# Opening loads and TensorE order of a fused attention and gated-FFN kernel: another load order, and a planner that prefers the tile shape that is on

## The chip, the cores and the metric

The kernel runs on one core of a Trainium2 chip. The metric is the device time of one execution in microseconds (us); lower is better. Before the change the median of three runs is 578.52 us (577.92 to 578.53). The five engines of the core are written as in the profile: PE (TensorE; PEld are its weight loads), DVE (VectorE), ACT (ScalarE), POOL (GpSimd) and SP (SyncE, which here only issues DMAs).

## The reference

All inputs are bfloat16; S = 2048 tokens, D = 576, 32 heads of 18, a window of 256 tokens, F = 4608.

```python
def _A_ref(x, wqkv, wo):                       # sliding-window attention
    qkv = (x @ wqkv).reshape(B, S, 3, H, Dh)   # ... to q, k, v by head
    scores = einsum("bhqd,bhkd->bhqk", q, k) * (Dh ** -0.5)
    mask = (idx[:, None] - idx[None, :] >= 0) & (idx[:, None] - idx[None, :] < W)
    p = softmax(where(mask, scores, -1e9))
    return einsum("bhqk,bhkd->bhqd", p, v) ... @ wo
def _B_ref(x, w_gate, w_up, w_down):           # gated FFN
    return (sigmoid(x @ w_gate) * (x @ w_up)) @ w_down

xn = layernorm(x)
return x + _A_ref(xn, wqkv, wo) * silu(_B_ref(xn, w_gate, w_up, w_down))
```

## The kernel before

The tokens are done in four chunks of 512 (`NCH`, `CH`), each of four tiles of 128 (`QPC`). The 576 features are split into nine blocks of 64 (`NC`), and most matmuls contract over 64 rows: two of them, one on the upper and one on the lower half of the array, run side by side. So PE works in four tile shapes, which the code calls modes: `full` (128 rows: the down projection F2, the transposes of the opening, the dummy matmuls), `r64` (64 rows: QKV projections, the output projection `wo`, gate and up matmuls F1), `r32` (32 rows: attention scores) and `c32` (32 columns: probabilities times V).

For a chunk the work is, by name: layer norm of four tiles (`bn1`, `bn2`, `ag`, `ve`, `rstd`, `apply`, `wrap`; lines 388 to 405, mostly DVE); the transposed normalised tile into `xn`, in chunk 0 by PE transposes `tr` (L424) and ACT copies `xe`, in later chunks by DMA transposes `xt`; twelve projections (`qk:c:i:0` is q of tile i, `qk:c:i:1` is k, `v:n` is v; L446, 18 matmuls each); for q and k an evacuation into a ring of three buffers `pk`, from which a DMA transpose `qkt` (L201) makes `qkp`; attention by eight groups of four heads (`sc` scores, L536; `pv`, L615); F1 for 36 tiles of 128 hidden features in weight groups of three (`fa:c:t`, `fb0`, `fb1`; L723, 18 matmuls per tile; the weights of group g are `w:c:g`, four DMAs); the output projection (`wo:c:0`, `wo:c:0s`, `wo:c:1`, `wo:c:1s`; L680); F2 for four token tiles in nine steps each (`f2:tile:step`; L791, in the last tile L821); and the final combination (`fth` on ACT, L852; `fq1`, `fq2`, `fq3` on DVE, L854 to L858), after which `out` is stored. `wo:c:0s` may start only when the results of `wo:c:0` have arrived (a fence), and `wo:c:1s` after `wo:c:1`. `fq2` of tile i needs `se` (L695), the ACT evacuation of its `wo`. Projection q of tile 3 (`qk:0:3:0`) writes a `pk` buffer that the transpose `qkt` of q of tile 2 must have read; `fa:0:3` is the first user of weight group 1.

Nothing of the order is written out by hand. `build` makes operations with dependencies, a priority, and a duration in ns that the author set by constants; `schedule` (L864) is a list planner: at each step it takes for every engine the operation with the least start time plus `prio * PRIO_NS`, and among the engines the earliest. The result is one fixed program per engine, and on the chip each engine runs its program strictly in that order, waiting on semaphores. So a changed constant moves no work by itself, but can give another order on every engine, SP included: SP issues all loads, stores and DMA transposes of the kernel, one after the other.

The constants that matter here: `MODE_NS` is added when PE goes to another mode (L957); `X_PRIO`, `QKV_LOAD` and `W0_PRIO` are the priorities of the opening loads (four tiles of x, twelve DMAs of `wqkv`, four of weight group 0); `W_FACTOR` scales the bytes that the planner counts for a `wqkv` load. `WARM` puts ten dummy matmuls (L327) at the start of PE's program, and `WARM_MORE` one more after the transposes of each of tiles 0 and 1. Loads of x for the final sum go into a ring of two buffers `xf` and wait for the store that empties the buffer; the planner adds `LATE_SLACK` (5000 ns) to their arrival.

Of the kernel before, what the change touches and what calls it, by code (L numbers as in the profile page):

```python
# [8 lines left out]
D = 576  # L9
# [3 lines left out]
P = 128  # L13
# [17 lines left out]
NC = D // 64  # L31
# [3 lines left out]
RW = 3  # L35
# [26 lines left out]
SEM_NS = 50.0  # L62
DMA_SLACK_NS = 600.0
PE_TAIL = 166.0
MODE_NS = 112.0
BEGIN_NS = 800.0
DMA_ISSUE_NS = 440.0
W_ISSUE_NS = 660.0
# [3 lines left out]
LN_STEP = 1  # L72
WARM = 10
X0_SLACK = 0.0
WARM_MORE = (1, 1)
X_PRIO = (-9, -9, -7, -5)
QKV_LOAD = (-8, -4, -6)
W0_PRIO = -3
WARM_NS = 427.0
W_FACTOR = 1.35  # L80
XT_BYTES = 1.6
DMA_LAT_NS = 1600.0
DMA_BYTES_PER_NS = 320.0
# [21 lines left out]

class Op:
    __slots__ = ("eng", "occ", "lat", "deps", "fn", "name", "prio", "start", "done", "tok",
                 "needs_tok", "nbytes", "idx", "slack", "succs", "cidx", "odeps", "alloc", "mode", "lane", "fence")

    def __init__(self, eng, occ, fn, name, deps, prio, nbytes=0, odeps=(), alloc=(), mode=None, lane=None):  # L110
        self.eng = eng
        self.occ = float(occ)
        self.lat = {"PE": PE_TAIL, "ACT": 110.0, "DVE": 85.0, "POOL": 50.0, "SP": 0.0}[eng]
        self.fn = fn
        self.name = name
        self.deps = []
        for d in deps:
            self.add_dep(d)
        self.prio = prio
        self.start = None  # L120
        self.done = None
        self.tok = None
        self.needs_tok = False
        self.nbytes = nbytes
        self.idx = -1
        self.succs = []
        self.odeps = [d for d in odeps if d is not None]
        self.alloc = list(alloc)
        self.mode = mode
        self.lane = lane  # L130
        self.fence = None

    def add_dep(self, d):
        if d is None:
# [27 lines left out]
class Builder:  # L162
# [156 lines left out]
        self.warm(WARM, "warm:0", [self.op_pre])  # L319
        self.op_pkz = op("ACT", 1300 + 1900, lambda e: e.memzero(self.pk[:, :, :, :]), "pkz", prio=0)  # L320

    def warm(self, n, name, deps, odeps=()):
        ps = Psum((3,))

        def f(e):
            for k in range(n):
                r = e.matmul(self.bank(ps), self.hT[:, 0, 0:P], self.hT[:, 0, :], start=True, stop=True)  # L327
            return r
        self.op_warm = self.pe(n * WARM_NS, f, name, deps=deps, prio=-9, psum=[ps], odeps=odeps)

    def load9(self, low, up, w_low, w_up, name, lane, deps, prio, factor=1.55):
        cols = w_low.shape[1]
# [39 lines left out]
    def build_ln(self, c):  # L372
        op = self.op
        pr = 0 if c == 0 else 2
        _, dxn = self.r_xn.take()
        self.op_xn = [[] for _ in range(QPC)]
        for i in range(QPC):
            st = c * QPC + i
            if c == 0:
                pr = LN_STEP * (i - QPC)  # L380
            ring, buf = (self.r_xf, self.xf) if c == 0 and i >= NXR else (self.r_xr, self.xr)
            sx, dx = ring.take()
            xs = buf[:, sx, :]
            o_x = self.dma(xs, self.x[st * P:(st + 1) * P, :], P * D * 2, f"x{st}",
                           ("x", i if c == 0 else sx), deps=dx + ([self.op_f1[(c - 1, 6 + 3 * i)]] if c > 0 else []),
                           prio=X_PRIO[i] if c == 0 else 4, slack=X0_SLACK if c == 0 else LATE_SLACK)
            sb_, db_ = self.r_bn.take()
            b1 = op("DVE", 360, lambda e, sb_=sb_, xs=xs: e.bn_stats(self.bnst[:, sb_, 0, :], xs[:, 0:288]),  # L388
                    f"bn1:{st}", deps=[o_x] + db_, prio=pr)
            b2 = op("DVE", 360, lambda e, sb_=sb_, xs=xs: e.bn_stats(self.bnst[:, sb_, 1, :], xs[:, 288:576]),  # L390
                    f"bn2:{st}", deps=[o_x] + db_, prio=pr)
            ag = op("DVE", 120, lambda e, st=st, sb_=sb_: e.bn_aggr(self.mv[:, st, :], self.bnst[:, sb_, :, :]),
                    f"ag:{st}", deps=[b1, b2], prio=pr)
            self.r_bn.release(sb_, ag)
            ve = op("DVE", 100, lambda e, st=st: e.tensor_scalar(self.veps[:, st, :], self.mv[:, st, 1:2], EPS,
                                                                None, ALU.add), f"ve:{st}", deps=[ag], prio=pr)
            rs = op("POOL", 560, lambda e, st=st: e.tensor_tensor(self.rstd[:, st, :], self.veps[:, st, :],  # L397
                                                                 self.neghalf[:, :], ALU.pow),
                    f"rstd:{st}", deps=[ve, self.op_negh], prio=0)
            sr, dr = self.r_xnr.take()  # L400
            ap = op("DVE", 350, lambda e, st=st, xs=xs, sr=sr: e.tensor_scalar(
                self.xnr[:, sr, 0:D], xs, self.mv[:, st, 0:1], self.rstd[:, st, :],
                ALU.subtract, ALU.mult), f"apply:{st}", deps=[rs, ag] + dr, prio=pr)
            ring.release(sx, ap)
            wr = op("DVE", 100, lambda e, sr=sr: e.tensor_copy(self.xnr[:, sr, D:DP], self.xnr[:, sr, 0:64]),
                    f"wrap:{st}", deps=[ap], prio=pr)
            tok = slice(i * P, (i + 1) * P)
            if c > 0:
                for k, (i0, i1, col) in enumerate(((0, NKT, 0), (NKT, NC, 64))):
                    o = self.dma(self.xn[:, i0:i1, tok], self.xnr[:, sr, col:col + (i1 - i0) * P],  # L410
                                 XT_BYTES * (i1 - i0) * P * P * 2, f"xt:{st}.{k}", ("xt", i, k), deps=[wr, ap] + dxn,
                                 prio=-2, issue=XT_ISSUE_NS, transpose=True)
                    self.r_xnr.release(sr, o)
                    self.op_xn[i].append(o)
                continue
            halves = [(0, NKT, 0), (NKT, NC, 64)]
            for i0, i1, col in halves:
                n = i1 - i0
                ps = Psum((4,), (5,), (6,), (7,), (0,), (1,), (2,), (3,))

                def f_tr(e, sr=sr, ps=ps, n=n, col=col):
                    b = ps.banks[0] * 1024
                    for k in range(n):
                        r = e.transpose(self.psb[:, b + k * P:b + (k + 1) * P],  # L424
                                        self.xnr[:, sr, col + k * P:col + (k + 1) * P], self.op_[:, NOT - 1, 0:P])
                    return r
                tr = self.pe(n * 58, f_tr, f"tr:{st}", deps=[wr, ap, self.op_ident] + dxn, prio=pr, psum=[ps])
                self.r_xnr.release(sr, tr)

                def f_xe(e, i=i, ps=ps, i0=i0, n=n):  # L430
                    b = ps.banks[0] * 1024
                    src = self.psb[:, b:b + n * P].rearrange("p (k c) -> p k c", k=n)
                    return e.activation(self.xn[:, i0:i0 + n, i * P:(i + 1) * P], src, ACTF.Copy)
                if i < len(WARM_MORE) and i1 == NC:
                    self.warm(WARM_MORE[i], f"warm:{i + 1}", [], [tr])
                self.op_xn[i].append(self.rd("ACT", act_ns(n * P), f_xe, f"xe:{st}", deps=[tr], prio=pr, psum=[ps]))
        self.all_xn = [o for l in self.op_xn for o in l]

# [76 lines left out]
    def build_attn(self, c, hg):  # L515
# [7 lines left out]
        masks = []  # L523
        for u, pieces in enumerate(units):
# [3 lines left out]
            ps = Psum((0, 1, 2, 3))  # L528
# [15 lines left out]
            pend = self.pending if u == PV_WITH else None  # L544
            if pend:
                self.pending = None
                o = self.pe(pend[1] + MODE_NS + nblk * P / 2.4 + 40, lambda e, a=pend[0], b=f_sc: (a(e), b(e))[1],
                            f"pvsc:{c}:{hg}:{u}", deps=pend[2] + deps, prio=0, psum=[pend[3], ps], mode=("c32", "r32"))
                pend[4](o)
            else:  # L550
                o = self.pe(nblk * P / 2.4 + 40, f_sc, f"sc:{c}:{hg}:{u}", deps=deps, prio=1, psum=[ps], mode="r32")
            self.op_sc[c][hg].append(o)
            exps = []
            for pr in range(2):
# [53 lines left out]
        def f_pv(e, ps=ps, where=where):  # L608
# [7 lines left out]
                                 self.expr[:, es, j, pos * P:(pos + n) * P], start=(m == 0), stop=(m == len(runs) - 1),  # L616
                                 tile_position=(0, 32 * j))
            return r
        self.pending = (f_pv, ncol / 2.4 + 40, masks + vdeps, ps, lambda o: self.after_pv(c, hg, ps, o, used))
        if hg == NHG - 1:  # L620
            o = self.pe(ncol / 2.4 + 40, f_pv, f"pv:{c}:{hg}", deps=masks + vdeps, prio=0, psum=[ps], mode="c32")
            self.pending[4](o)
            self.pending = None

# [75 lines left out]
    def build_ffn(self, c):  # L700
# [25 lines left out]
        for ft in range(NFT + 1):  # L726
            if ft < NFT:
                if ft % FG == 0:
                    fg = ft // FG
                    sw, dw = self.r_w.take()  # L730
                    slots.append(sw)
                    wp = (fg + 1 if fg else W0_PRIO) if c == 0 and fg < RW else -2
                    fc = slice(fg * FG * P, (fg + 1) * FG * P)
                    dmas.append(self.load9(self.wgs[0:64, sw, :, :], self.wgs[64:P, sw, :, :], self.wg[:, fc],
                                           self.wu[:, fc], f"w:{c}:{fg}", ("w", sw),
# [128 lines left out]
    def schedule(self):  # L864
# [14 lines left out]
        mode = "full"  # L879
# [31 lines left out]
        while n < total:  # L911
            best = None
            for e in ENGS:
                bo = None
                for o in enabled[e]:
                    st = max(free[e], ready[o.cidx])
                    pen = o.prio * PRIO_NS
                    if o.alloc:
                        if bo is not None and (st + pen, o.cidx) >= bo[0]:
                            continue  # L920
# [175 lines left out]
```

## Time and profile before

| what | before |
|---|---|
| median of three runs (lowest, highest) | 578.52 us (577.92, 578.53) |
| the profiled execution: its time, its span | 579.13 us, 577.1 us |
| PE busy | 568.1 us, 98% of the span |
| ACT, DVE, POOL busy | 303.3, 296.2, 24.4 us |
| F1 matmuls (L723) | 2592, 298.9 us busy |
| F2 matmuls (L791) | 1080, 135.8 us busy |
| projections (L446) | 864, 55.6 us busy |
| DMA traffic | 72.82 MB, mean 126 GB/s, 58.4% of 16 engines |

The span runs from the first to the last instruction of the profiled execution; the 2.0 us between it and that execution's time lie around it. The busy time of PE counts overlapping matmuls once, and the ends of matmuls are modelled, so a short wait or a change of tile shape does not show as idle time: start-to-start times have to be read instead. In the views below the columns are start, duration, engine, line, operation, destination and sources, count, and in brackets the idle time before it with what ended it.

### The profile page before, as it was taken

Reading aid. Unit: us, or ns where it says so; the run is one execution under the profiler, and the core shown is the slowest. Engines: PE = TensorE matmul, PEld = TensorE weight load, DVE = VectorE, ACT = ScalarE, POOL = GpSimd, SP = SyncE. Lnnn points to the kernel's source line nnn. Section 1 sums busy time; section 2 is a strip of 40 time slices with the busy share of each in tenths; the row PEclk is TensorE's granted clock in tenths of the full one; section 3 lists DMA queues with packets and bytes.
Section 4 is the critical chain, followed back from the end, with each engine's and each line's share of the span. In section 5 each row is a group of like instructions: output and inputs, shape, how many; then the busy total and the mean of one; then the engine's idle time right before and its main releaser. Section 6 shows DMA issues by size and latency. Waiting matters only on the chain.

```text
span 577.1 us, 14818 instructions
## 1 busy us (share of the span) xinstructions
PE 568.1 (98%) x6352; PEld 273.9 (47%) x6352; DVE 296.2 (51%) x589; ACT 303.3 (53%) x411; POOL 24.4 (4%) x51
## 2 busy tenths in 40 slices
PE   7999999999999999999999999999999999999996
PEld 4544334447544444455754444445564444444554
DVE  5237988403147887721225698761312677675012
ACT  5357887213168788530327878742133878882201
POOL 2001110000001010000000011000000000000000
PEclk9999999999999999999999999999999999999999
DMA  8999889634956664342693656544179356551010
GB/s 196 202 202 243 215 205 206 158 51 77 220 88 145 144 155 120 77 87 51 112 217 70 141 128 146 124 100 83 31 164 191 73 124 135 136 124 42 1 41 22
DMA packets 124861, 72.82 MB, mean 126 GB/s; under 512 B 53630, under 2 KB 124286, under 8 KB 124798
## 3 DMA queue, kind: packets, MB, share of 16 engines
q1 hardware_dynamic: 124798, 71.90, 58.4%
q8 instruction: 50, 0.82, 0.6%
q14 instruction: 13, 0.11, 0.1%
HBM read 55.22 MB, written 2.36 MB: 100 GB/s over the span
## 4 chain that ended last, share of the span: by engine, by line
PE 95%; DMA 2%; SPq 2%; DVE 1%; issue 0%; POOL 0%; ACT 0%
PE ps L723 50%; PE ps L791 23%; PE ps L446 8%; PE ps L536 5%; PE ps L615 4%; PE ps L680 3%; PE ps L821 2%; SPq L202 1%; DMA qkp<-pk 1%; DMA xf<-in_A_x_dram 1%; DVE pk L488 0%; SPq L201 0%; PE ps L424 0%; POOL rstd L397 0%; DVE bnst L388 0%
## 5 line engine op out<-in xcount | busy, mean ns | idle before, releaser
L723 PE MATMUL ps<-xn,wgs 64*128 64x512 bf16 x2592 | 298.9, 377 | 0.3 <-ACT pk L489 0.3
L558 ACT ACTIVATE expr<-ps 128x1024 bf16<-128x1024 f32 (+2 forms) x192 | 175.8, 968 | 39.9 <-PE ps L536 39.2
L723 PEld LDWEIGHTS ps<-xn,wgs 64*128 64x128 bf16 x2592 | 119.7, 94 | 150.1 <-issue 15.1
L791 PE MATMUL ps<-wd_sb,hT 128*128 128x512 bf16 (+1 forms) x1080 | 135.8, 287 | 0.0
L709 ACT ACTIVATE tring<-ps 128x512 bf16<-128x512 f32 x144 | 86.3, 599 | 68.5 <-PE ps L723 65.8
L713 DVE SCALAR_TENSOR_TENSOR hT<-tring,ps 128x512 bf16<-128x512 bf16 x144 | 97.2, 675 | 39.4 <-ACT tring L709 26.3
L592 DVE TENSOR_TENSOR expr<-expr,m 128x1024 bf16<-128x1024 bf16 (+1 forms) x152 | 82.4, 572 | 59.6 <-ACT expr L558 59.4
L791 PEld LDWEIGHTS ps<-wd_sb,hT 128*128 128x128 bf16 x1080 | 67.9, 98 | 66.6 <-issue 4.1
L854 DVE SCALAR_TENSOR_TENSOR thf<-thf,ps 128x576 bf16<-128x576 bf16 (+2 forms) x17 | 12.2, 719 | 97.6 <-ACT thf L852 97.6
L852 ACT ACTIVATE thf<-ps 128x576 bf16<-128x576 f32 (+2 forms) x17 | 10.6, 623 | 90.5 <-PE ps L791 82.9
L446 PE MATMUL ps<-wqkv_sb,xn 64*128 64x288 bf16 x864 | 55.6, 283 | 0.2 <-DMA qkp<-pk 0.2
L446 PEld LDWEIGHTS ps<-wqkv_sb,xn 64*128 64x128 bf16 x864 | 41.3, 94 | 13.6 <-issue 1.7
L536 PE MATMUL ps<-qkp 18*128 18x384 bf16 (+2 forms) x704 | 36.8, 276 | 0.0
L488 DVE CAST pk<-ps 128x576 bf16<-128x576 f32 x16 | 12.1, 755 | 39.9 <-PE ps L446 39.9
L630 DVE STREAM_TRANSPOSE tf<-ps 128x512 f32<-128x512 f32 x32 | 22.9, 716 | 13.5 <-PE ps L536 10.4
L536 PEld LDWEIGHTS ps<-qkp 18*128 18x128 bf16 x704 | 11.1, 92 | 34.6 <-issue 20.2
L489 ACT ACTIVATE pk<-ps 128x576 bf16<-128x576 f32 x16 | 10.4, 652 | 30.4 <-PE ps L446 30.4
L615 PE MATMUL ps<-expr,vau 128*32 128x256 bf16 (+2 forms) x704 | 25.6, 277 | 0.0
L597 POOL COPY qkp<-qkp 128x256 bf16<-128x256 bf16 x24 | 11.7, 489 | 308.2 <-PE ps L536 308.2
L644 DVE STREAM_TRANSPOSE op__63<-pk 128x512 bf16<-128x512 bf16 x32 | 22.7, 709 | 1.3 <-DVE pk L638 0.5
L695 ACT ACTIVATE sat<-ps 128x576 bf16<-128x576 f32 x16 | 9.2, 654 | 21.5 <-PE ps L680 21.5
L615 PEld LDWEIGHTS ps<-expr,vau 128*32 128x32 bf16 x704 | 13.1, 96 | 15.4 <-ACT tring L709 7.6
(39 smaller groups left out, 157.1 us busy)
## 6 DMA issues: line engine op xcount, KB each, us to landing
wgs<-in_B_w_gate_dram SPq DMA_DIRECT2D x48, 240.0 KB, 3.8
wgs<-in_B_w_up_dram SPq DMA_DIRECT2D x48, 240.0 KB, 4.7
wgs<-in_B_w_up_dram SPq DMA_DIRECT2D x48, 192.0 KB, 4.1
wgs<-in_B_w_gate_dram SPq DMA_DIRECT2D x48, 192.0 KB, 4.6
wd_sb<-in_B_w_down_dram SPq DMA_DIRECT2D x9, 576.0 KB, 5.0
xf<-in_A_x_dram SPq DMA_DIRECT2D x18, 144.0 KB, 2.3
out_dram<-xf SPq DMA_DIRECT2D x15, 144.0 KB, 2.0
xr<-in_A_x_dram SPq DMA_DIRECT2D x14, 144.0 KB, 4.4
```

Of the source, the lines that this page charges most:

```text
L446: r = e.matmul(self.bank(ps, HV, hf), self.xn[r0:r0 + 64, k, i * P:(i + 1) * P], self.wqkv_sb[r0:r0 + 64, j, k, :], start=(k == 0), stop=( ...
L536: r = e.matmul(self.ps[:, b:b + n * P], self.qkp[r0:r0 + DH, hg, k0:k0 + P], self.qkp[r0:r0 + DH, hg, q0 * P:(q0 + n) * P], start=True, st ...
L558: return e.activation(self.expr[:, es, 2 * pr:2 * pr + 2, 0:nblk * P], src, ACTF.Exp, scale=SM_SCALE)
L592: return e.tensor_tensor(ap, ap, m, ALU.mult)
L615: r = e.matmul(self.ps[32 * j:32 * j + 32, b + q0 * P:b + (q0 + n) * P], vf[:, v0:v0 + 32], self.expr[:, es, j, pos * P:(pos + n) * P], st ...
L630: t1 = self.rd("DVE", dve_ns(CH), lambda e, ps=ps: e.transpose(tf.rearrange("p g d -> p (g d)"), self.bank(ps)), f"t1:{c}:{hg}", deps=[o_p ...
L644: t2 = self.op("DVE", dve_ns(CH), lambda e, on=on: e.transpose(self.op_[:, hg % NOT, :], on.rearrange("p g d -> p (g d)")), f"t2:{c}:{hg}" ...
L680: r = e.matmul(self.bank(ps2[w], n1 - n0, n), self.oT[r0:r0 + 64, kt, qi * P:(qi + 1) * P], self.wo_sb[r0:r0 + 64, kt, n0:n1], start=(swap ...
L709: return e.activation(self.tring[:, st_, :], self.bank(ps), ACTF.Tanh, scale=0.5)
L713: return e.scalar_tensor_tensor(self.hT[:, ft, :], self.tring[:, st_, :], 1.0, self.bank(ps), ALU.add, ALU.mult)
L723: return e.matmul(self.bank((pg, pu)[gu][ft]), self.wgs[r0:r0 + 64, slots[ft // FG], i, fl * P:(fl + 1) * P], self.xn[r0:r0 + 64, i, :], s ...
L791: r = e.matmul(self.ps[:, b + n0:b + n1], lhsT, self.wd_sb[:, q, fl, n0:n1], start=(ft == 0), stop=(ft == NFT - 1))
```

## The change

Four things change, all in what the planner is told. The opening loads get other priorities: all four tiles of x first, then q, v, weight group 0, k. The two extra dummy matmuls (`WARM_MORE`) go. The durations given to the planner change: 94 ns instead of 112 for a change of mode, 10 ns less for each score and `pv` operation, factors of 1.55 for `wqkv` loads and 1.7 for x tiles 2 and 3. And `KEEP_NS`: when PE's mode is `full` or `r64`, an operation of the other of these two modes (the transposes excepted) is put back by 100 ns in the choice.

```diff
-MODE_NS = 112.0
+MODE_NS = 94.0
+KEEP_NS = 100.0
...
-WARM_MORE = (1, 1)
-X_PRIO = (-9, -9, -7, -5)
+X_PRIO = (-9, -9, -9, -9)
 QKV_LOAD = (-8, -4, -6)
-W0_PRIO = -3
+W_PRIO = (-5, 2, 3)
 WARM_NS = 427.0
-W_FACTOR = 1.35
+W_FACTOR = 1.55
+X0_FACTOR = 1.7
...
+        self.keep = mode in ("full", "r64")
...
-            o_x = self.dma(xs, self.x[st * P:(st + 1) * P, :], P * D * 2, f"x{st}",
+            o_x = self.dma(xs, self.x[st * P:(st + 1) * P, :], (X0_FACTOR if c == 0 and i > 1 else 1.0) * P * D * 2, f"x{st}",
...
                 tr = self.pe(n * 58, f_tr, f"tr:{st}", deps=[wr, ap, self.op_ident] + dxn, prio=pr, psum=[ps])
+                tr.keep = False
...
-                if i < len(WARM_MORE) and i1 == NC:
-                    self.warm(WARM_MORE[i], f"warm:{i + 1}", [], [tr])
...
-                o = self.pe(pend[1] + MODE_NS + nblk * P / 2.4 + 40, ...
+                o = self.pe(pend[1] + MODE_NS + nblk * P / 2.4 + 30, ...
...
-                o = self.pe(nblk * P / 2.4 + 40, f_sc, ...
+                o = self.pe(nblk * P / 2.4 + 30, f_sc, ...
...
-                    wp = (fg + 1 if fg else W0_PRIO) if c == 0 and fg < RW else -2
+                    wp = W_PRIO[fg] if c == 0 and fg < RW else -2
...
                     pen = o.prio * PRIO_NS
+                    if e == "PE" and o.keep and mode in ("full", "r64") and o.mode != mode:
+                        pen += KEEP_NS
```

More of the change, by code (lines that the diff above doesn't have):

```diff
@@ L107 @@
     __slots__ = ("eng", "occ", "lat", "deps", "fn", "name", "prio", "start", "done", "tok",
-                 "needs_tok", "nbytes", "idx", "slack", "succs", "cidx", "odeps", "alloc", "mode", "lane", "fence")
+                 "needs_tok", "nbytes", "idx", "slack", "succs", "cidx", "odeps", "alloc", "mode", "lane", "fence", "keep")
     def __init__(self, eng, occ, fn, name, deps, prio, nbytes=0, odeps=(), alloc=(), mode=None, lane=None):
@@ L320, in build_init, with warm @@
         self.op_pkz = op("ACT", 1300 + 1900, lambda e: e.memzero(self.pk[:, :, :, :]), "pkz", prio=0)
-    def warm(self, n, name, deps, odeps=()):
+    def warm(self, n, name, deps):
         ps = Psum((3,))
@@ L328, in f @@
             return r
-        self.op_warm = self.pe(n * WARM_NS, f, name, deps=deps, prio=-9, psum=[ps], odeps=odeps)
+        self.op_warm = self.pe(n * WARM_NS, f, name, deps=deps, prio=-9, psum=[ps])
     def load9(self, low, up, w_low, w_up, name, lane, deps, prio, factor=1.55):
@@ L546, in build_attn @@
                 self.pending = None
-                o = self.pe(pend[1] + MODE_NS + nblk * P / 2.4 + 40, lambda e, a=pend[0], b=f_sc: (a(e), b(e))[1],
+                o = self.pe(pend[1] + MODE_NS + nblk * P / 2.4 + 30, lambda e, a=pend[0], b=f_sc: (a(e), b(e))[1],
                             f"pvsc:{c}:{hg}:{u}", deps=pend[2] + deps, prio=0, psum=[pend[3], ps], mode=("c32", "r32"))
@@ L550, in build_attn @@
             else:
-                o = self.pe(nblk * P / 2.4 + 40, f_sc, f"sc:{c}:{hg}:{u}", deps=deps, prio=1, psum=[ps], mode="r32")
+                o = self.pe(nblk * P / 2.4 + 30, f_sc, f"sc:{c}:{hg}:{u}", deps=deps, prio=1, psum=[ps], mode="r32")
             self.op_sc[c][hg].append(o)
@@ L618, in f_pv @@
             return r
-        self.pending = (f_pv, ncol / 2.4 + 40, masks + vdeps, ps, lambda o: self.after_pv(c, hg, ps, o, used))
+        self.pending = (f_pv, ncol / 2.4 + 30, masks + vdeps, ps, lambda o: self.after_pv(c, hg, ps, o, used))
         if hg == NHG - 1:
-            o = self.pe(ncol / 2.4 + 40, f_pv, f"pv:{c}:{hg}", deps=masks + vdeps, prio=0, psum=[ps], mode="c32")
+            o = self.pe(ncol / 2.4 + 30, f_pv, f"pv:{c}:{hg}", deps=masks + vdeps, prio=0, psum=[ps], mode="c32")
             self.pending[4](o)
```

## The prediction

> **What bounds the kernel now.** I read the page first: busy times and the chain of waits that ended last.
>
> ```profile
> span 577.1 us, 14818 instructions
> PE 568.1 (98%) x6352; PEld 273.9 (47%) x6352; DVE 296.2 (51%) x589; ACT 303.3 (53%) x411; POOL 24.4 (4%) x51
> ...
> PE 95%; DMA 2%; SPq 2%; DVE 1%; issue 0%; POOL 0%; ACT 0%
> ```
>
> PE bounds it: 95% of the chain. PE's work hardly changes (two dummy matmuls go), so a gain can come only from waits and from changes of tile shape. The waits show as idle time of PE, all in the opening, next in the timeline of PE:
>
> ```profile
> 1.50 4.26 PE L327 MATMUL ps<-hT 128*128 128x512 bf16 x10 [1.50 <-DVE neghalf L304]
> 6.09 0.68 PE L424 MATMUL ps<-op__63,xnr 128*128 128x128 bf16 x9 [0.32 <-DVE xnr L405]
> ...
> 10.82 0.68 PE L424 MATMUL ps<-op__63,xnr 128*128 128x128 bf16 x9 [0.63 <-DVE xnr L405]
> 11.43 2.38 PE L446 MATMUL ps<-wqkv_sb,xn 64*128 64x288 bf16 x36
> 15.37 0.68 PE L424 MATMUL ps<-op__63,xnr 128*128 128x128 bf16 x9 [1.56 <-DVE xnr L405]
> 15.98 3.48 PE L446 MATMUL ps<-wqkv_sb,xn 64*128 64x288 bf16 x54
> ```
>
> PE waits 0.63 and 1.56 us for tiles 2 and 3 of x, loaded behind q and v (tile 3 issued at 7.75, landed 4.45 us later, by the chain). F1 starts at 19.40 us, with seven projections (q of three tiles, v of four) done. The timeline of SP tells why weight group 1 matters:
>
> ```profile
> 13.67 5.36 SPq L201 DMA_TRANSPOSE qkp<-pk  x2
> 19.07 0.62 SPq L202 DMA_DIRECT2D wgs<-in_B_w_gate_dram  x1
> 19.73 0.62 SPq L202 DMA_DIRECT2D wgs<-in_B_w_up_dram  x1
> 20.39 1.33 SPq L201 DMA_TRANSPOSE qkp<-pk  x1
> 21.77 0.60 SPq L202 DMA_DIRECT2D wgs<-in_B_w_gate_dram  x1
> 22.41 0.62 SPq L202 DMA_DIRECT2D wgs<-in_B_w_up_dram  x1
> ```
>
> Two transposes hold SP until 19.0 (asked one by one: 1.53 and 3.78 us), while the loads before them land (the last of group 0 at 13.01 + 6.3 = 19.3). The last load of group 1, issued at 22.41, lands 6.0 us later, at 28.4. The last view, F2 of chunk 0, prices a change of tile shape:
>
> ```profile
> 114.32 1.40 PE L680 MATMUL ps<-wo_sb,oT 64*128 64x512 bf16 x20
> 115.65 1.16 PE L791 MATMUL ps<-wd_sb,hT 128*128 128x512 bf16 x8
> 116.74 1.15 PE L680 MATMUL ps<-wo_sb,oT 64*128 64x512 bf16 x16
> 117.83 2.13 PE L791 MATMUL ps<-wd_sb,hT 128*128 128x512 bf16 x16
> 119.89 1.40 PE L680 MATMUL ps<-wo_sb,oT 64*128 64x512 bf16 x20
> ```
>
> The long stretch of F2 (216 matmuls from 537.15 to 563.62) gives 0.245 us for a 512-column matmul with its 64-column partner. Eight matmuls are 0.98 us and take 1.09 from start to start; sixteen are 1.96 and take 2.06. A change costs about 0.105 us.
>
> **The opening.** SP's new order is x0 to x3, q, v, group 0, k, then three transposes of q instead of two, then group 1 whole. So x2 passes four DMAs and x3 eight, q is put back by two x loads, and k by the four of group 0. An x load takes 0.46 us of issue alone (0.79 to 1.25), the others 0.655. Nearly the same DMAs precede the first transpose, so it is issued near 13.4 and the third at 19.07 as the second lets go. Step by step:
>
> Tiles 2 and 3 now arrive near 4 and 5 us. DVE's new program puts their statistics ahead of the first `apply`, which is bad for tiles 0 and 1: two of 0.37 us start to start and one aggregate (0.2), less the 0.31 us that DVE now idles for POOL, move `wrap` of tile 0 from 5.85 to 6.5, and the first transpose to 6.75; tile 1 starts 7.4. The half projection q0 (0.49 us) starts at 7.95. Tile 2 follows at 8.9, tile 3 at 10.3 (statistics 7.25, `apply` 9.6, `wrap` 10.05). q's last load, landed at 3.81 + 3.6 = 7.4 before, is put back by about 0.9, to 8.3, ahead of its use at 9.5. Then PE has the rest of q0, q1, q2 and four v: a projection is 1.10 us (180 matmuls from 133.30 to 144.43). From 10.9 that ends at 17.5, with v landed near 12 (x3 landed behind the same bytes at 12.20) and group 0 near 16.5: twelve plus the 4.5 us that it took after k before (10.36 + 4.4 = 14.8 to 19.3). F1 starts at 17.5 against 19.40, with the same seven projections done: **-1.9**.
>
> Next come 34 F1 matmuls, k0, four more, k1, q3, fourteen more; with 0.2156 us for a pair (36 matmuls take 3.99, 18 take 2.05, start to start) and two unpaired at first, PE reaches `fa:0:3` at 26.6 and asks for group 1. Its loads are issued from 20.4 to 22.4, all behind the transpose. The first should lag as the one at 19.07 did, 3.9 us: 24.3. The others follow at the rate of the windows from 21 to 27 us, 220 to 226 GB/s, 0.98 us for a mean load of 216 KB: the last lands at 27.2, a wait of 0.6. Before, the waits from 19.40 to the first scores at 37.49 add to 0.85 (18.09 less 106 F1 matmuls, five projections, one change); they are gone where k and q3 find their buffers read. New scores: 36.4, with ten F1 matmuls (1.08) more done. In all 37.49 - 36.4 + 1.08 = **-2.1**. Ends: no wait, -2.7; group 1 as late as before (28.4), -0.9. I take the value nearest to the queue's own rows. The two dummy matmuls lie in this sum.
>
> Behind it, `pvsc:0:1:1` needs two exponentials (L558, mean 968 ns) and two masks (L592, 572 ns) with only 30 F1 matmuls to hide them: **+0.1**, from 0 to one more activation (L709, 0.6).
>
> **The tile shapes.** Counted in the built programs, PE changes shape 221 times instead of 229. From chunk 0's F1 to chunk 1's it is 11 instead of 21, since `wo` is no longer cut into F2 but lies beside the projections: 10 x 0.105 = **-1.05** (-0.8 to -1.2). In chunks 1 and 2 the count is equal: `wo:c:0` stands within F1, `wo:c:1` among projections. There `wo:c:1` and F2 hold six of eight PSUM banks, so k of tile 3 needs the evacuation of q of tile 3 (L488, 755 ns, and its signals) under the 0.98 us of `wo:c:1s`: **+0.1** for both (0 to 0.4).
>
> In chunk 0 the transpose of k of tile 3 is put behind the four loads of group 4; in chunk 1 it stays behind twelve loads while its scores come sooner. By the same rates both land about 1.5 us before their scores, under F1 and F2 matmuls; I cost them at nothing, and where that cover is short, scores and all behind them on PE wait for the difference.
>
> **The end.** In chunk 3 `wo:3:1` and `wo:3:1s` move between F2 of tiles 14 and 15: two more changes (+0.2) and an uncovered fence. ACT starts 0.20 us after the next group (563.82 against 563.62), so +0.2 (0.1 to 0.4). Worse, DVE's order becomes `fq3:15:0` after both smaller `fq1` and `fq2`, because the planner counts the x load behind `out13` as late. Before:
>
> ```profile
> 571.86 0.39 DVE L856 TENSOR_TENSOR thf<-thf,sat 128x448 bf16<-128x448 bf16 x1
> 572.29 0.39 DVE L858 TENSOR_TENSOR xf<-xf,thf 128x448 bf16<-128x448 bf16 x1
> 572.95 0.29 DVE L854 SCALAR_TENSOR_TENSOR thf<-thf,ps 128x128 bf16<-128x128 bf16 x1 [0.27 <-ACT thf L852]
> 573.27 0.23 DVE L856 TENSOR_TENSOR thf<-thf,sat 128x128 bf16<-128x128 bf16 x1
> 573.53 0.23 DVE L858 TENSOR_TENSOR xf<-xf,thf 128x128 bf16<-128x128 bf16 x1
> ```
>
> On these times `fq3:15:0` moves from 572.29 to 573.53, the last one to 573.95; the first store is issued then, the second 0.38 behind it, 0.55 later than the 573.78 of before. x15 itself comes in time: `out13` about 2 us after tile 15's start, landed in 1.7 to 3.7, the load 2.1 more, against 9.9. **+0.55**; with the rest +0.95 (0.6 to 1.2).
>
> **Sum.** -2.1 + 0.1 - 1.05 + 0.1 + 0.95 = -2.0. The profiled execution (span 577.1, 2.0 around it, 579.13) becomes 577.1; it stands 0.6 above the median, so the median becomes **576.5**. The ends add to -3.3 and +0.5: 575.2 to 579.0.
>
> **The clock.** The first ten dummies take 0.426 us each, twice the later 0.2156: PE begins at half speed. After PE's end the granted clock is 1.00 from 573 to 575 and 0.62 from 575 to 577, so it halves some 2.9 us after the last matmul. My longest gap is 1.0 us and the clock should hold.
>
> [...]
>
> **Rivals.** (a) The opening's gain is eaten: group 1 at 28.4 and the unfavourable ends of the small waits (0.6, 0.4): -0.9 + 0.6 - 1.05 + 0.4 + 0.95 = 0, 578.5. For it: three DMA-bound steps in a row; against: the queue is drained at 19.3. (b) Slower: SP is held by the third transpose as by the second, 3.78 us. Group 1 is then issued from 22.9 to 24.9 and, with its lag of 6.0, lands at 30.9 instead of 27.2: +3.7, so 580.2. It makes the kernel slower from a landing at 29.2 on. For it: transposes at 15.24 (3.78) and 26.14 (2.82) were held; against: those had weight loads outstanding, and the one at 20.39 took 1.33 with two. [...] (d) No wait for group 1, and none behind: -2.7 - 1.05 + 0.95 = -2.8, 575.7.
>
> **Chances.** Forecast 0.45, (a) 0.22, (b) 0.12, (c) 0.08, (d) 0.13. What this measurement can tell from no change is 0.2%, 1.16 us. Faster: 0.38 of the forecast, (d), 0.05 of the others: 0.56. Slower: (b) and 0.04: 0.16. The rest, 0.28, is the same. The range, 575.0 to 579.2, leaves out (b) and some tails; the forecast's own is 575.7 to 577.5.
>
> **What would show it.** F1 (L723) starting at 17 to 18; PE idle before it near 27 for weights; first scores near 36.4; one run of projections with `wo` after 18 steps of F2; the last store 0.5 later after the last matmul than before. Group 1 landing after 29, projections at half speed before 14, or scores of chunk 1 or 2 waiting for transposes would prove me wrong.

## The result, and the profile after

| | before | after |
|---|---|---|
| median (lowest, highest) of 14 runs each | 578.82 us (577.92, 580.94) | 577.42 us (577.06, 577.8) |
| ratio, 95% interval | | 0.9975 [0.9967, 0.9983] |
| the profiled execution: its time, its span | 579.13 us, 577.1 us | 577.34 us, 575.3 us |

The change makes the kernel faster by 0.25%: 1.4 us by the medians, 1.8 us by the two profiled executions. Below, every figure called "against before" is a difference of two profiled executions at the start of the same matmul, so that a gain and its loss can be found in place. (The weight load in front of a matmul does not serve for this: it starts 0.21 us ahead of its matmul where PE runs through, as at 236.64 in after, and together with it behind a change of tile shape, as at 239.48 in before.) The page of the kernel after, its busy times and the shares of the chain of waits:

```profile
span 575.3 us, 14816 instructions
PE 567.7 (99%) x6350; PEld 274.0 (48%) x6350; DVE 294.8 (51%) x589; ACT 303.6 (53%) x411; POOL 23.0 (4%) x51
...
PE 95%; SPq 1%; DMA 1%; DVE 1%; ACT 0%; issue 0%; DVEq 0%
```

PE is still the bound, with nearly the same busy time (567.7 against 568.1 us); the gains and losses have to be looked for in the waits and the changes of tile shape. The opening in PE's timeline:

```profile
1.51 4.45 PE L329 MATMUL ps<-hT 128*128 128x512 bf16 x10 [1.51 <-DVE neghalf L306]
6.28 1.72 PE L426 MATMUL ps<-op__63,xnr 128*128 128x128 bf16 x18 [0.33 <-DVE xnr L407]
...
9.87 0.68 PE L426 MATMUL ps<-op__63,xnr 128*128 128x128 bf16 x9
10.47 6.79 PE L447 MATMUL ps<-wqkv_sb,xn 64*128 64x288 bf16 x108
17.10 3.83 PE L724 MATMUL ps<-xn,wgs 64*128 64x512 bf16 x33
...
26.86 6.00 PE L724 MATMUL ps<-xn,wgs 64*128 64x512 bf16 x54 [0.46 <-DMA wgs<-in_B_w_up_dram]
32.68 2.38 PE L447 MATMUL ps<-wqkv_sb,xn 64*128 64x288 bf16 x36
34.89 1.26 PE L724 MATMUL ps<-xn,wgs 64*128 64x512 bf16 x10
36.08 0.34 PE L537 MATMUL ps<-qkp 18*128 18x384 bf16 x4
```

The waits of 0.63 and 1.56 us for tiles 2 and 3 are gone, six projections run in one piece, and F1 starts at 17.10 instead of 19.40. Then PE stands idle for 0.46 us, waiting for weight group 1; from start to start it loses 0.62, since the matmul before it starts at 26.02 and needs 0.216 (single records). The first scores come at 36.08 instead of 37.49, with ten more F1 matmuls done. SP's timeline shows what group 1 stands behind:

```profile
10.75 2.60 SPq L204 DMA_DIRECT2D wqkv_sb<-in_A_wqkv_dram  x4
13.40 6.05 SPq L203 DMA_TRANSPOSE qkp<-pk  x3
19.49 0.60 SPq L204 DMA_DIRECT2D wgs<-in_B_w_gate_dram  x1
20.14 0.66 SPq L204 DMA_DIRECT2D wgs<-in_B_w_up_dram  x1
20.84 1.40 SPq L204 DMA_DIRECT2D wgs<-in_B_w_gate_dram  x1
22.28 0.62 SPq L204 DMA_DIRECT2D wgs<-in_B_w_up_dram  x1
```

Three transposes hold SP for 2.82, 1.83 and 1.31 us (by their single records). The last load of group 1 is issued at 22.28 and lands, by its completion in the trace, at 26.72; before it was issued at 22.41 and landed at 28.38. The next view is PE's timeline at the boundary from chunk 0 to chunk 1:

```profile
125.87 11.20 PE L447 MATMUL ps<-wqkv_sb,xn 64*128 64x288 bf16 x180
137.03 4.59 PE L681 MATMUL ps<-wo_sb,oT 64*128 64x512 bf16 x72
141.47 2.38 PE L447 MATMUL ps<-wqkv_sb,xn 64*128 64x288 bf16 x36
143.78 1.15 PE L792 MATMUL ps<-wd_sb,hT 128*128 128x512 bf16 x8
```

`wo` is one piece among the projections, in the same tile shape, where before it was cut four times into F2. Last, PE's timeline of the end, and then that of all engines (PE's weight loads, ACT, DVE, SP) from the last `wo` on:

```profile
532.16 26.64 PE L792 MATMUL ps<-wd_sb,hT 128*128 128x512 bf16 x216
558.73 2.62 PE L681 MATMUL ps<-wo_sb,oT 64*128 64x512 bf16 x36
561.28 8.99 PE L822 MATMUL ps<-wd_sb,hT 128*128 128x448 bf16 x72
```

```profile
560.19 0.85 PEld L681 LDWEIGHTS ps<-wo_sb,oT 64*128 64x128 bf16 x16 [0.37 <-PE ps L681]
...
569.53 0.39 DVE L857 TENSOR_TENSOR thf<-thf,sat 128x448 bf16<-128x448 bf16 x1
570.31 0.28 ACT L853 ACTIVATE thf<-ps 128x128 bf16<-128x128 f32 x1 [1.47 <-PE ps L822]
570.62 0.29 DVE L855 SCALAR_TENSOR_TENSOR thf<-thf,ps 128x128 bf16<-128x128 bf16 x1 [0.69 <-ACT thf L853]
570.94 0.22 DVE L857 TENSOR_TENSOR thf<-thf,sat 128x128 bf16<-128x128 bf16 x1
571.09 0.52 DVE L859 TENSOR_TENSOR xf<-xf,thf 128x448 bf16<-128x448 bf16 x2
571.50 0.81 SPq L204 DMA_DIRECT2D out_dram<-xf  x2
```

Half of `wo:3` now lies between F2 of tiles 14 and 15, with an uncovered fence (0.37 us at PE's weight loads), and the large addition `fq3:15:0` (128x448, ready at 569.92, when the `fq2` before it ends) stands behind the two smaller steps of the 128-column rest, at 571.09, so both stores go out together at the very end. Set side by side, start of the matmul in us (F1 matmul 541 of a chunk is the first of its tile 30; behind it the chunk has only F1, `wo` and what follows):

| matmul | before | after | against before |
|---|---|---|---|
| first scores (after has ten F1 matmuls, 1.08, more done) | 37.49 | 36.08 | -2.50 |
| F2 of chunk 0 | 110.30 | 108.13 | -2.17 |
| F1 matmul 541 of chunk 1 | 239.71 | 236.64 | -3.07 |
| F1 matmul 541 of chunk 2 | 380.24 | 377.32 | -2.92 |
| F1 matmul 541 of chunk 3 | 520.77 | 517.99 | -2.78 |
| F2 of tile 15 | 563.62 | 561.28 | -2.33 |
| end of the span | 577.13 | 575.32 | -1.81 |

So the opening brings 2.5 us and the boundary of chunks 0 and 1 0.90; 0.33 goes at the first softmax, 0.15 in each of chunks 1 and 2, 0.44 before tile 15 and 0.52 behind it.

### The profile page after: what moved, and what is told of

The parts are those of the page before. It is cut to its first block, busy times and chain, and to the rows that moved or that the text cites. A ratio compares the mean times of both kernels' runs of the same rounds, so it can differ in the third digit from the quotient of the medians.

```text
span 575.3 us, 14816 instructions
## 1 busy us (share of the span) xinstructions
PE 567.7 (99%) x6350; PEld 274.0 (48%) x6350; DVE 294.8 (51%) x589; ACT 303.6 (53%) x411; POOL 23.0 (4%) x51
## 4 chain that ended last, share of the span: by engine, by line
PE 95%; SPq 1%; DMA 1%; DVE 1%; ACT 0%; issue 0%; DVEq 0%
PE ps L724 50%; PE ps L792 23%; PE ps L447 8%; PE ps L537 5%; PE ps L616 4%; PE ps L681 3%; PE ps L822 2%; SPq L203 1%; DMA wgs<-in_B_w_up_dram 1%; PE ps L426 1%; SPq L204 0%; DMA xr<-in_A_x_dram 0%; DVE bnst L390 0%; DVE bnst L392 0%; DVE pk L489 0%
## 5 line engine op out<-in xcount | busy, mean ns | idle before, releaser
L710 ACT ACTIVATE tring<-ps 128x512 bf16<-128x512 f32 x144 | 86.3, 599 | 74.0 <-PE ps L724 71.3
L681 PE MATMUL ps<-wo_sb,oT 64*128 64x512 bf16 (+1 forms) x288 | 19.8, 283 | 0.1
```

The costliest lines, as they stand in the source:

```text
L681: r = e.matmul(self.bank(ps2[w], n1 - n0, n), self.oT[r0:r0 + 64, kt, qi * P:(qi + 1) * P], self.wo_sb[r0:r0 + 64, kt, n0:n1], start=(swap ...
L710: return e.activation(self.tring[:, st_, :], self.bank(ps), ACTF.Tanh, scale=0.5)
```

## The experiments

Nine kernels ran. All compute the whole reference. Ratios are to the kernel before, timed beside each on the same chip.

**The new loads alone.** The kernel after, with the planner's constants for tile shapes and scores set back:

```diff
-MODE_NS = 94.0
-KEEP_NS = 100.0
+MODE_NS = 112.0
+KEEP_NS = 0.0
...  (scores and pv: + 40 instead of + 30)
```

> The changed opening (loads, no extra dummies, its order of PE up to the first scores), with the planner's mode constants as before, so that wo is cut into F2 again and the end is as before. By my sum the opening gains 2.1 us of PE time (the changed kernel's profile says 2.5: first scores at 36.07 instead of 37.49, with ten more F1 matmuls done, 1.08 us) and gives 0.1 to 0.3 back at the first softmax: the time is 2.0 to 2.3 us below the kernel before, a ratio near 0.9963, and better than the whole change. Rival, that the opening's gain is given back later in chunk 0 and the ordering rule brings the change's gain: ratio 0.999 to 1.001.

Measured: 576.92 us, ratio 0.9961 [0.9947, 0.9974], span 574.7. PE starts F1 and waits for group 1 as in after:

```profile
24.72 1.67 PE L724 MATMUL ps<-xn,wgs 64*128 64x512 bf16 x12
26.90 6.00 PE L724 MATMUL ps<-xn,wgs 64*128 64x512 bf16 x54 [0.51 <-DMA wgs<-in_B_w_up_dram]
...
36.12 0.34 PE L537 MATMUL ps<-qkp 18*128 18x384 bf16 x4
```

There is no wait at the first softmax, and the gain of 2.46 us stands unchanged from F2 of chunk 0 over F1 matmul 541 of chunks 1 to 3 to tile 15 (561.15) and the end. The loads (with the two dummies left out) carry all of the kernel's gain, and what is lost behind the opening is lost by the new order.

**The tile-shape preference alone.** The kernel before with the other half of the change:

```diff
-MODE_NS = 112.0
+MODE_NS = 94.0
+KEEP_NS = 100.0
...  (keep in the planner's choice, scores and pv + 30)
```

> The ordering part alone (94 ns for a change of mode, the preference for the mode that is on, 10 ns less for scores and pv), with the loads and dummies of before. By my sum it gains 1.05 us at the boundary of chunks 0 and 1 and pays 0.1 to 0.3 in chunks 1 and 2 and 0.95 to 1.15 at the end: between -0.1 and +0.4 us, a ratio of 0.9998 to 1.0007, no gain. Rival, that fewer changes of shape is what makes the changed kernel faster: -0.8 us or more, ratio 0.9986 or less.

Measured: 578.88 us, ratio 0.9998 [0.999, 1.0007], span 577.3. Against before it is 0.15 us ahead at the first scores, 1.05 at F1 matmul 541 of chunk 1 (238.66), 0.76 at that of chunk 3, 0.32 at tile 15 (563.30), and 0.2 behind at the end. The preference wins 0.9 us at one boundary and gives 0.3 back in chunks 1 and 2 and 1.0 at the end of the kernel.

**The output projection of chunk 3 out of F2.** The kernel after, with an order (no wait) that keeps `wo:3` behind F1 of tile 36, where before had it:

```diff
+            self.wo_first = (self.wo_first if pair[0] else []) + [wa]
...
+        if c == NCH - 1:
+            for wa in self.wo_first:
+                wa.odeps.append(oa)
```

> The changed kernel with one more order edge: in chunk 3 the output projection starts after the last F1 step, as before the change. By my sum the end's terms go (two changes of shape, the fence, the late last store): 1.15 us below the changed kernel, about 2.6 us below the kernel before, ratio near 0.9955; tile 15's F2 starts about 0.65 us earlier, and the span ends 13.5 us after that start as before instead of 14.0. Rival, that wo in the middle of F2 is free because its waits lie beside DVE's and ACT's work: ratio 0.9975, as the changed kernel.

Measured: 576.28 us, ratio 0.9951 [0.9939, 0.9964], span 574.0; the interval lies wholly below that of after. The end in PE's timeline:

```profile
529.28 4.76 PE L681 MATMUL ps<-wo_sb,oT 64*128 64x512 bf16 x70
534.20 26.41 PE L793 MATMUL ps<-wd_sb,hT 128*128 128x64 bf16 x211 [0.16 <-issue]
560.44 8.98 PE L826 MATMUL ps<-wd_sb,hT 128*128 128x448 bf16 x72
```

F2 runs through into tile 15 without `wo`, and the span ends 13.51 us after tile 15 starts, as before (13.52), against 14.04 in after. Against before it is 3.17 us ahead at F1 matmul 541 of chunk 3, at tile 15 and at the end: both losses at the end, 0.96 together, hang on that one placement. (The other 0.4 by which its span is shorter than after's came in its opening, with the first scores at 35.69.)

**The last addition alone.** The kernel after, with the planner told that the last load of x for the final sum comes in time (PE's order is the same as in after):

```diff
-  deps=dx + [self.op_hT[NFT - 6]], prio=3, slack=LATE_SLACK)
+  deps=dx + [self.op_hT[NFT - 6]], prio=3, slack=DMA_SLACK_NS if sb == NQB - 1 else LATE_SLACK)
```

> The changed kernel, only the planner's lateness for the load of x tile 15 cut from 5000 to 600 ns, so that DVE does fq3 of the large part of tile 15 ahead of the small part again; nothing on PE moves. By my sum 0.5 us below the changed kernel (the last store is issued 0.5 us sooner after the last matmul), ratio near 0.9966. Rival, that this x load, behind the store of tile 13, really lands late: then fq3 waits for it, and the time is that of the changed kernel, 0.9975, or above.

Measured: 577.12 us, ratio 0.9964 [0.9952, 0.9976], span 575.2. DVE's timeline has the large addition ahead of the small steps again:

```profile
570.39 0.39 DVE L859 TENSOR_TENSOR xf<-xf,thf 128x448 bf16<-128x448 bf16 x1
571.05 0.29 DVE L855 SCALAR_TENSOR_TENSOR thf<-thf,ps 128x128 bf16<-128x128 bf16 x1 [0.27 <-ACT thf L853]
571.37 0.22 DVE L857 TENSOR_TENSOR thf<-thf,sat 128x128 bf16<-128x128 bf16 x1
571.63 0.23 DVE L859 TENSOR_TENSOR xf<-xf,thf 128x128 bf16<-128x128 bf16 x1
```

Tile 15 starts at 561.71 and the span ends 13.53 us later: 0.5 us is the price of the order of four DVE instructions. The interval overlaps that of after; only the profile shows it, since this execution opened 0.4 later than after's (first scores 36.52), which hides the half microsecond in the span.

**The two halves of the load order, each on the kernel before.** First x alone, then group 0 alone:

```diff
-X_PRIO = (-9, -9, -7, -5)
+X_PRIO = (-9, -9, -9, -9)
```

> The kernel before with one edit: all four tiles of x are loaded first. My theory is that the two halves of the new load order need each other: PE then has its seven projections done near 17.5, but weight group 0 still comes behind k and lands near 19.3, so F1 starts at 19.2 to 19.5 as before and the gain is 0 to 0.8 us (waits further on), ratio 0.9986 to 1.000. Rival, that x alone was the bound: F1 starts near 17.5 and the ratio is 0.9965 or less.

```diff
-W0_PRIO = -3
+W0_PRIO = -5
```

> The kernel before with one priority changed, so that weight group 0 is loaded before k (x tiles 2 and 3 stay behind q and v). Together with the run that moves x alone it shows both halves of the new load order. Theory 1 (the two halves need each other): group 0 lands near 15.5 instead of 19.3, but PE still waits for tiles 2 and 3 of x and has its seven projections done no sooner, so F1 starts at 19.0 to 19.4 as before; where the first scores come sooner it is by at most 0.8 us, ratio to before 0.9986 to 1.000. Theory 2 (the weights alone carry the opening's gain): F1 starts near 17.5 with fewer projections done, first scores near 36.1 or as many more F1 matmuls done, ratio 0.9965.

Measured: x alone 578.92 us, ratio 0.9998 [0.999, 1.0007]; group 0 alone 579.02 us, 0.9999 [0.999, 1.0008]. PE's timeline with x alone:

```profile
10.54 6.79 PE L446 MATMUL ps<-wqkv_sb,xn 64*128 64x288 bf16 x108
19.09 1.88 PE L723 MATMUL ps<-xn,wgs 64*128 64x512 bf16 x15 [1.77 <-DMA wgs<-in_B_w_up_dram]
```

The projections are done as early as in after, and PE then waits 1.77 us for group 0. With group 0 alone:

```profile
11.46 2.38 PE L446 MATMUL ps<-wqkv_sb,xn 64*128 64x288 bf16 x36 [0.23 <-DMA wqkv_sb<-in_A_wqkv_dram]
14.98 0.68 PE L424 MATMUL ps<-op__63,xnr 128*128 128x128 bf16 x9 [1.14 <-DVE xnr L405]
15.59 3.48 PE L446 MATMUL ps<-wqkv_sb,xn 64*128 64x288 bf16 x54
18.91 1.89 PE L723 MATMUL ps<-xn,wgs 64*128 64x512 bf16 x15
```

The wait for tile 3 of x stays (1.14 us), and F1 starts at 18.91. The scores come 0.9 us sooner, but with eight F1 matmuls fewer behind them, and F2 of chunk 0 starts at 110.25, as before (110.30). Neither half gains in the medians; only both at once remove the wait. The run with x alone is not quite nothing: in its profile it stands 0.9 us ahead of before from the first scores to the end, and four of its eleven times (577.79 to 578.12) lie below all 29 of before that were taken beside it (from 578.21 on), while the other seven lie at 578.81 to 579.94. So it gains in some executions; no run shows what decides that.

**The dummy matmuls.** The kernel after with the two extra ones back, and with none at all:

```diff
+WARM_MORE = (1, 1)
...
+                if i < len(WARM_MORE) and i1 == NC:
+                    self.warm(WARM_MORE[i], f"warm:{i + 1}", [], [tr])
```

> The changed kernel with the two extra dummy matmuls put back. Theory 1: the opening ends at the wait for weight group 1 (0.46 us), so 0.43 us of dummies is hidden there: time as the changed kernel within 0.3 us, ratio 0.997 to 0.998, F1 starting later and its wait for group 1 smaller. Theory 2: without the dummies the clock rises later (7.5 us in the changed kernel's profile, 5.5 in that of before), and putting them back gains: ratio under 0.997 and a clock that rises near 5.5. Theory 3: the dummies cost what they last: 0.4 us more, ratio 0.9983.

```diff
-        self.warm(WARM, "warm:0", [self.op_pre])
```

> The changed kernel without any dummy matmul, so that the first work of PE is the transposes near 6.3 us. [...]

Measured: with both back 577.51 us (576.97 to 581.0), ratio 0.999 [0.9977, 1.0003], too scattered to decide by time. In its profile F1 starts at 17.10, as in after, but the granted clock was full from 5.76 on, against 7.46 in after; in the two profiles without these dummies where it was full by 6.12 (`wo:3` moved back; the last experiment below), F1 starts at 16.70 and 16.68. So the two dummies put F1 back by some 0.4 us, and that costs nothing: the first F1 matmul of group 1 still waits 0.2 us for its weights, from start to start, and the first scores come at 35.67, sooner than in after. With none 578.83 us, ratio 1.0 [0.9991, 1.0009], all of the gain gone in the medians. PE's timeline of that kernel:

```profile
6.22 2.10 PE L425 MATMUL ps<-op__63,xnr 128*128 128x128 bf16 x18 [6.22 <-DVE xnr L406]
8.25 1.14 PE L446 MATMUL ps<-wqkv_sb,xn 64*128 64x288 bf16 x8
9.32 0.90 PE L425 MATMUL ps<-op__63,xnr 128*128 128x128 bf16 x9
10.15 0.79 PE L446 MATMUL ps<-wqkv_sb,xn 64*128 64x288 bf16 x10
...
18.11 1.24 PE L723 MATMUL ps<-xn,wgs 64*128 64x512 bf16 x10
```

The eighteen transposes take 2.10 us and the half projection 1.14 instead of 0.66: PE is slower until 9.83, where the stretch at full speed begins in the trace's record of the granted clock. F1 starts 1.0 us later than in after. But this execution was the fastest of its ten (578.07; the slowest 579.30), and its span of 576.2 us is still 0.9 below that of before. In it PE again waits for group 1, whose last load landed at 27.49, 0.8 later than in after, and the first scores are later by just that; whether the missing dummies cause the late landing, and what the slower executions lose beyond it, no trace shows.

**Both gains, without the losses.** The loads of the first experiment with `KEEP_NS`, and `wo` of chunks 1 to 3 kept behind F1:

```diff
-KEEP_NS = 0.0
+KEEP_NS = 100.0
...
+        if c > 0:
+            for wa in self.wo_first:
+                wa.odeps.append(oa)
```

> The changed opening and the preference for the mode that is on, with the planner's mode constants as before (112, and 10 ns more for scores and pv), and with wo of chunks 1 to 3 held until F1 of its chunk has ended. If the profile's terms are separate and add, it keeps -2.5 (opening) and -1.1 (chunks 0 to 1) and drops the wait at the first softmax, the 0.15 in each of chunks 1 and 2 and the end's terms: 3.5 us below the kernel before, ratio near 0.994, about 575.5 us. Rival, that the terms eat each other, since the opening and chunk 0 share their DMA time: no better than the run with wo of chunk 3 alone moved, 0.995.

Measured: 575.87 us (575.26 to 576.23), ratio 0.9948 [0.9936, 0.996], span 573.9: faster than both kernels, and not told apart from the third experiment's. Two rows of PE's timeline say why it gained 3.2 us in the profile (2.24 in the opening, 0.96 at the boundary, nothing lost behind) and not the 3.5 expected:

```profile
6.18 1.23 PE L426 MATMUL ps<-op__63,xnr 128*128 128x128 bf16 x18 [0.41 <-DVE xnr L407]
...
27.12 3.20 PE L725 MATMUL ps<-xn,wgs 64*128 64x512 bf16 x28 [1.14 <-DMA wgs<-in_B_w_up_dram]
```

In this execution the first transposes already ran at full speed (1.23 us for eighteen, 1.72 in after) and F1 started 0.4 us sooner, yet PE then waited 1.14 us for group 1 and had its scores at 36.33, later than after's. What comes out of the opening is set by the landing of group 1, not by the work ahead of it. The seven profiles with the new loads show it, in us:

| run | third transpose lets SP go | last load of group 1 lands | first scores |
|---|---|---|---|
| two dummies back | 18.98 | 26.31 | 35.67 |
| `wo:3` behind F1 | 19.08 | 26.33 | 35.69 |
| after | 19.45 | 26.72 | 36.08 |
| loads alone | 19.50 | 26.76 | 36.12 |
| both gains | 19.80 | 26.98 | 36.34 |
| last addition | 19.91 | 27.17 | 36.52 |
| no dummies | 19.49 | 27.49 | 36.85 |

The first scores follow the landing by 9.36 us in all seven, while F1 starts anywhere from 16.68 to 18.11. The landing follows the moment at which SP is let go by 7.2 to 7.3 us in six of them, and by 8.0 without dummies.

## Why the prediction was right, step by step

The forecast, faster by the sum of an opening gain and a boundary gain less a loss at the end, is what the profile and the experiments show, and the time lies in its range, 0.9 us above the value named. Its terms, in us:

| term | predicted | measured | shown by |
|---|---|---|---|
| the opening | -2.1 | -2.5 | table; loads alone -2.46 |
| first softmax | +0.1 | +0.33 | table; 0 with the loads alone |
| boundary of chunks 0 and 1 | -1.05 | -0.90 | table; preference alone -0.90 |
| chunks 1 and 2 | +0.1 | +0.29 | table; 0 with the loads alone |
| end: `wo:3` in F2 | +0.4 | +0.44 | table; gone when `wo:3` is moved back |
| end: last store | +0.55 | +0.52 | 14.04 against 13.52 (before) and 13.53 (last addition) |
| sum | -2.0 | -1.8 | spans 577.13 and 575.32 |

That the sum came within 0.2 us is in part luck: the opening gave 0.4 more than its term, and the three terms behind it together 0.6 less.

**The opening** was put 0.4 too low. The first transpose came at 6.28, not 6.75: in DVE's timeline of after, the two statistics of tile 2 lie where DVE had waited for POOL, and `apply` starts at 5.60, only 0.21 later than before; I had let them push it by 0.65:

```profile
5.23 0.45 DVE L392 BATCH_NORM_STATS2 bnst<-xf 128x6 f32<-128x288 bf16 x1
5.60 0.41 DVE L403 TENSOR_SCALAR xnr<-xr,mv,rstd 128x576 bf16<-128x576 bf16 x1
```

That gave F1 at 17.1 instead of 17.5, of which nothing counts by itself, as the seven profiles above show. What counts is group 1: the third transpose let SP go at 19.45, not 20.4, and the last load landed at 26.72, not 27.2. The wait, 0.62 us from start to start for a predicted 0.6, came out right because PE and the weights were early by nearly as much.

**The small waits.** The place of the first softmax wait was named rightly, at `pvsc:0:1:1`, and the 0.33 lies within the range I gave it (0 to 0.6). The timeline of after has it:

```profile
49.30 1.03 DVE L593 TENSOR_TENSOR expr<-expr,m 128x1024 bf16<-128x1024 bf16 x2 [2.07 <-ACT expr L559]
50.23 0.60 ACT L710 ACTIVATE tring<-ps 128x512 bf16<-128x512 f32 x1 [0.47 <-PE ps L724]
50.88 0.68 PE L616 MATMUL ps<-expr,vau 128*32 128x384 bf16 x16 [0.26 <-ACT tring L710]
```

What ended it was not the step that the term was worked out from: the two masks are done at 50.33, before PE falls idle at 50.62, and PE goes on when an F1 activation (L710) ends at 50.83. That activation stood only at the upper end of my range.

The 0.15 in each of chunks 1 and 2 is in the table, but no run separated the PSUM evacuation that I named from the other moves at these boundaries; that cause stays open.

**The boundary** gave 0.90 for ten changes of shape, 0.09 each where the stretches of F2 had given 0.105; that lies within the range of the term. No run separates the ten.

**The end** went as worked out: 0.44 for two more changes and the fence, put at 0.4, and 0.52 for the last store, put at 0.55. How the 0.44 divides between changes and fence is not measured; the 0.37 us at the weight loads is idle time of the loads, not of the matmuls.

**From the profile to the median** lies most of the miss. The sum was 0.2 us off; but I let the changed kernel's median stand 0.6 below its profiled execution, as the three runs of before did. Fourteen runs put before's median at 578.82, 0.3 below its profiled execution, and after's median is 0.1 above its own. That offset belonged in the range and not in the time.

**The rivals.** (a) group 1 as late as before: it landed 1.7 us sooner than then. (b) SP held 3.78 us by the third transpose: it was held 1.31. (c) a halved clock in the opening, which had 0.08: no run shows one behind the rise. The record of the granted clock has one unbroken stretch at full speed in every profiled execution, until behind the last matmul. In after it begins at 7.46, so twelve of the first eighteen transposes began at half speed (0.107 us from start to start from 6.47 to 7.43, 0.056 from 7.51 on), which the prediction did not consider; in before it begins 3.96 us after the first of the dummies. In the run without dummies the clock was full 3.6 us after the first transposes, and the only other PE work until then, 1.1 us of projection, had begun 1.6 us before it, while in the ten executions with dummies the rise came 2.8 to 6.0 us after PE's first matmul. The run without dummies was profiled once, and what raised the clock in it was not shown. (d) no wait for group 1: it came to pass in none of the seven profiles with the new loads. From start to start PE waits 0.2 us with the two dummies back, too short to show as idle time, and 0.4 to 1.3 in the others.

## What to carry to other kernels

Where two loads gate a stage one behind the other, move both or neither: neither half alone moved the median, both together gave 0.4%. A preference that a planner applies everywhere (keep the tile shape that is on) should be read at each place where it acts: here one boundary gained 0.9 us, and the last stage lost as much to a single misplaced block; an ordering edge put it back and made the best kernels of the study. And when the last load is the limit, as group 1 is here, faster work ahead of it only lengthens the wait: of the 0.68 us by which it is longer with both gains than in after, 0.42 are F1's earlier start.

## What the runs showed of the hardware

- The clock did not rise at a fixed time. With the same ten dummies from 1.5 us on, it is full from 4.34 us in the earliest of ten profiled executions and from 7.50 in the latest (before 5.46, after 7.46), a spread of 3.16 us; the eighteen first transposes take 1.23 us where it is early (both gains) and 1.72 in after. The stretch at full speed was 566.61 us long in seven of eleven records (the one without dummies among them) and 570.03 in the other four.
- A DMA transpose can hold the queue that issues it for longer than a load, which in most cases takes 0.62 us: 2.82, 1.83 and 1.31 us for three in a row in after, 1.53, 3.78 and 1.33 in before. Of the first six transposes in each of the eleven profiles, those that begin with one or two earlier loads still to land take 1.31 to 1.34 us, and those with four or more 1.34 to 3.78. Loads asked for behind them are issued later by as much.
- The same loads in the same order do not land at the same time: the last of group 1 lands from 26.31 to 27.49 in the seven profiles with the new loads, and most of that spread is there already when the third transpose lets SP go (18.98 to 19.91). These 1.2 us are most of the change's whole gain, so one profile of this opening settles no question below it.
